# Edges that hold attention steps in chunks 1 to 3, the fifth chunk's scores from chunk 2 on, and coarse pieces of chunk 1 at tiles 1, 3, 5 and 7

## The chip, the cores and the metric

The kernel runs on one core of a Trainium2 chip. The metric is the device time of one execution in microseconds (us). The kernel before takes 1087.3 us, the median of three runs (1086.87, 1087.3 and 1091.65).

## The reference

Two kinds of attention over q, k and v (8 batches, 8 heads, 576 positions, 64 wide) are added, and a gated feed-forward network (FFN) with an RMS norm ahead of it runs on the 4608 tokens.

```
q_d, k_d, v_d = means of q, k, v over 4 neighbours           # 144 positions
out_up    = repeat(softmax(q_d k_d^T / 8) v_d, 4)            # "coarse"
scores    = where(|i - j| < 4, q k^T / 8, -1e9)              # a band, 7 wide
out_local = softmax(scores) v                                # "local"
x   = (out_up + out_local) as [4608, 512]
xn  = x / sqrt(mean(x^2) + 1e-6) * rms_g
g   = xn @ w_gate;  val = xn @ w_val                         # 512 -> 1536
out = (g * sigmoid(g) * val) @ w_out                         # 1536 -> 512
```

## The kernel before, in words

**Chunks and tiles.** The tokens are cut into 18 chunks of 256, numbered 0 to 17. The FFN of a chunk runs in 12 tiles of 128 columns of `w_gate` and `w_val`. "Tile c.f" is tile f of chunk c. Each fp32 operand is split into a high and a low part. For each tile TensorE runs 24 matmuls of the first product (L1344: 12 for `wg`, 12 for `wv`, each four triples of one `xl` and two `xh` matmuls) and, two tiles later, 6 of the second (L1380). Between them stand tanh on ScalarE (L1352), gate (L1355) and product (L1360) on VectorE (DVE), the high part on ScalarE (L1366) and the low part on DVE (L1369). Three buffers `sil` and three `hs` lie between first and second product.

**The input of a chunk.** The tokens of chunks 0 to 2 come from `Dense`, which does the band on TensorE; its root is at L1231 to L1246 and its norm at L1252. The tokens of chunks 3 to 17 come from `Attention`, mostly on DVE. In code order these are its steps:

- eight scores, each a product (L711) and a sum (L715) on DVE, with loads of `q_t` and `kv` on SP's queue (L699, L617);
- the softmax (L732 to L749), with one exponential on ScalarE;
- eight values: the seven neighbours' products are split between ScalarE (L758), DVE and GpSimd (both L765; GpSimd is POOL in the profile), and a sum on DVE (L784);
- twice an "add": `load_up` (L794, two DMAs on ScalarE's queue) brings the coarse result, `add_up` (L800) adds it on DVE, and the squares (L810) run on ScalarE;
- the root: a mean over partitions on TensorE (L817), then eleven or twelve small operations on DVE (L821 to L840) and the norm (L849);
- the turn: transposes on TensorE (L861), and `xh` (L300, ScalarE) and `xl` (L304, DVE), which the first matmul of the next chunk waits for.

**Coarse pieces.** The coarse attention runs in pieces of one batch and one pair of heads. Each has scores on TensorE (L534), maxima, a subtraction and a reciprocal on DVE (L555, L560, L596, L599), exponentials on ScalarE (L565), a turn (L574) and values (L589) on TensorE, and a scale (L603) with a store (L606). Their inputs are summed by chains of accumulating DMAs on GpSimd's queue (L372), which SP loads (L364, L368). Chunk 1 has four pieces, the later ones two each; a piece needs a tile for its scores, and turn and values follow two and three tiles later.

**What sets the order.** Chunk 0 is planned by a planner of its own. Chunks 1 to 17 are emitted by the loop at L1518 to L1559, and a list scheduler orders the instructions of each engine. Within chunk c the loop emits, for each tile, the FFN tile, then queued steps (root at tile 8, turn at tile 10) and coarse pieces, and then the steps of `Attention(c + 1)` whose place in tiles has come (`todo`; scores from 0 to 2.6, softmax at 3.0, values from 3.1 to 6.0, adds at 4.8 and 6.4). What is emitted is free to be placed earlier by the scheduler: nothing but data and buffers holds a step of `todo`. `tc.issue_after(x)` adds an edge: what is traced inside it comes after x on the engines. Before, only queued steps, coarse pieces and second products carry such edges.

In the trace of before, the first matmul of chunk 1 runs at about 145 us; chunks 2, 3 and 4 begin at about 216, 277 and 336.

Of the kernel before, what the change touches and what calls it, by code (L numbers as in the profile page):

```python
# [13 lines left out]
AF = mybir.ActivationFunctionType  # L14
# [15 lines left out]
NF = DF // P  # L30
# [11 lines left out]
FIRST = 1  # L42
WARM = 2
V_ROWS = 50.0
PIECES = {1: (1, 4, 6, 8), 2: (0, 3), 3: (0, 2)}
SUMS = {(1, 6): (3, 0), (1, 11): (3, 2)}


HOP = {"PE": 0.25, "ACT": 0.2, "DVE": 0.15, "POOL": 0.2, "SP": 0.0}
# [127 lines left out]
def attn_moe_kernel(  # L177
# [16 lines left out]
    nc = tc.nc  # L194
# [258 lines left out]
    def behind(ins):  # L453
        return tc.issue_after(ins) if ins else nullcontext()
# [3 lines left out]
    def sums_of(b, hp):  # L458
        if (b, hp // 2) not in sums:
            sums[b, hp // 2] = Sums(b, hp // 2)  # L460
        return sums[b, hp // 2]
# [821 lines left out]
    class Forward:  # L1283
# [6 lines left out]
        def emit(self, f):  # L1290
            self.first(f, 0)
            last = self.first(f, 1)
            self.tanh(f)
            self.gate(f)
            self.product(f)
            self.high(f)
            self.low(f, "DVE")
            return last

        def emit_second(self, f):  # L1300
# [7 lines left out]
        def plan(self, weights, second_weights):  # L1308
            att, c, T = self.att, self.c, due[self.c]
            o_bufs = [buf("ps_o") for _ in range(2)]  # L1310
            last = None
            for f in range(NF):
                at = T + 4.2 * f
                soon = at - SOON
                hp, sil, hs = buf("ps_h"), buf("sil"), buf("hs")
                x = [att.xh_buf, att.xl_buf]
                first = task(
                    "PE", 1.375, lambda f=f: self.first(f, 0), at, [*att.turned, *weights(f)], allocs=[hp], uses=x,
                )
                tanh = task("ACT", 0.38, lambda f=f: self.tanh(f), soon, [first], allocs=[sil], uses=[hp])  # L1320
                val = task("PE", 1.375, lambda f=f: self.first(f, 1), at, [first], uses=[hp, *x])
                gate = task("DVE", 0.415, lambda f=f: self.gate(f), soon, [tanh], uses=[hp, sil])
                prod = task("DVE", 0.415, lambda f=f: self.product(f), soon, [gate, val], uses=[hp, sil])
                high = task("ACT", 0.415, lambda f=f: self.high(f), soon, [prod], allocs=[hs], uses=[sil])
                low = task(
                    (("DVE", 0.42, soon), ("POOL", 0.95, soon)), 0, lambda e, f=f: self.low(f, e), soon, [high], uses=[sil, hs],
                    port=True,
                )
                last = task(
                    "PE", 1.375, lambda f=f: self.second(f), at + 4.2 * LAG, [low, last, *second_weights(f)],  # L1330
                    allocs=o_bufs if f == 0 else [], uses=[hs, *o_bufs],
                )
            for j in range(2):
                o_sb = buf("o_sb")
                copy = task("ACT", 0.6, lambda j=j: self.copy(j), T, [last], allocs=[o_sb], uses=[o_bufs[j]])
                task("SP", 0.1, lambda j=j: self.store(j), T, [copy], uses=[o_sb], dma=0.256 * MB)
# [12 lines left out]

        def tanh(self, f):  # L1350
            self.sil[f] = ffn.tile([P, C], FP32, name="sil", bufs=3)
            nc.scalar.activation(out=self.sil[f], in_=self.p[f][:, 0], func=AF.Tanh, scale=0.5)  # L1352

        def gate(self, f):
            nc.vector.scalar_tensor_tensor(  # L1355
                out=self.sil[f], in0=self.sil[f], scalar=1.0, in1=self.p[f][:, 0], op0=ALU.add, op1=ALU.mult,
            )

        def product(self, f):
            nc.vector.scalar_tensor_tensor(  # L1360
# [39 lines left out]
    for fg in range(3):  # L1400
        for i in range(12):
            if i % 3 == 2 if fg < 2 else i >= 8:
                f = 4 * fg + (i // 3 if fg < 2 else i - 8)
# [94 lines left out]
    early = Dense(2).plan_scores(parts, opening, mask, 24.0, 105.0)  # L1498
# [16 lines left out]

    att, late = atts[FIRST], []  # L1518
    for c in range(FIRST, NCH):
        todo, before, behind_second = [], {}, {}  # L1520
        if c + 1 < NCH:
            nxt = early if c == FIRST else Attention(c + 1)
            todo, queued = nxt.steps()
            todo.sort(key=lambda t: t[0])
            for at, it in zip(PIECES.get(c, (0, 3)), coarse[done:]):
                score, swap, value = Coarse(*it).steps()
                behind_second[at] = score
                before.setdefault(at + 2, []).append(swap)
                before.setdefault(at + 3, []).append(value)
                done += 1  # L1530
            for at, step in queued.items():
                before.setdefault(at, []).append(step)
        fwd = Forward(att)
        for f in range(NF):
            if (c, f) in SUMS:
                sums_of(*SUMS[c, f])
            if f in (0, 6) and c > FIRST:
                for it in coarse[done - 1:done + 1 if f else done]:
                    sums_of(*it)
            last = fwd.emit(f)  # L1540
            for step in before.get(f, ()):
                with behind(last):
                    last = step()
            late.append((fwd, f))
            if len(late) > LAG:
                fw, g = late.pop(0)
                with behind(last if f in before else None):
                    last = fw.emit_second(g)
            if f in behind_second:
                with behind(last):  # L1550
                    behind_second[f]()
            while todo and todo[0][0] < f + 1:
                todo.pop(0)[1]()
        assert not todo
        att = nxt
    assert done == len(coarse)
# [56 lines left out]
```

## Time and profile before

| | us |
|---|---|
| median of three runs | 1087.3 |
| the profiled execution | 1088.73 |
| its span in the profile | 1087.0 |
| outside the span | 1.7 |
| TensorE busy | 1044.5 (96%) |
| DVE busy | 887.4 (82%) |
| ScalarE busy | 626.4 (58%) |
| GpSimd busy | 168.0 (15%) |
| granted TensorE clock, mean | 0.983 |

In the lines of the trace, PE is TensorE, ACT ScalarE, POOL GpSimd and SP the queue of most loads. A line of the timeline has the start (us from the span's start), the busy time, the engine, the source line, the operation, its output and inputs by the program's names, shapes, and how many instructions (x) stand behind one another. In brackets is the idle time ahead of it, and what ended it. A line of the waits has the waiting engine and line, whom it waited for, the sum in us, how often, and the longest. A row of windows has the window, its length, then busy time and count for PE, PEld, DVE, ACT and POOL, the granted clock, DMA share and GB/s.

### The profile page before, as it was taken

To read this page: it belongs to the slowest core of one execution; us is meant where nothing else is said; L and a number is where in the kernel's file an instruction comes from. 1 tells how busy PE (TensorE), PEld (TensorE's weight loads), DVE (VectorE), ACT (ScalarE), POOL (GpSimd) and SP (SyncE) were. 2 spreads that over 40 slices of the span, in tenths; PEclk is the share of its full clock that TensorE was granted. 3 is DMA by queue.
4 is the path that set the end of the run, shared out by engine and by line. 5 is a ranking of instruction groups with operands and counts; after the bars stand their busy time and mean duration, and the time that the engine had idled before them with its cause. 6 is when DMAs were issued, how large, how long until landed. Compare 5 with 4: busy or idle time off the path is not lost.

```text
span 1087.0 us, 23815 instructions
## 1 busy us (share of the span) xinstructions
PE 1044.5 (96%) x8804; PEld 958.7 (88%) x8804; DVE 887.4 (82%) x1988; ACT 626.4 (58%) x2308; POOL 168.0 (15%) x225
## 2 busy tenths in 40 slices
PE   4888899899999999999999999999999999999998
PEld 2667799689998999999999999999999999999997
DVE  5778859885979998989898898989899998986432
ACT  5588743843747483848384838384738383746222
POOL 3201300312121121212121212020202010111000
PEclk8888999999999999999999999999999999999999
DMA  8488842564362635353535353313132222210000
GB/s 264 135 277 309 223 116 75 116 160 83 91 130 63 134 94 118 85 119 87 126 81 123 77 129 81 97 41 106 43 105 61 82 86 65 84 40 21 1 21 20
DMA packets 72731, 113.28 MB, mean 104 GB/s; under 512 B 26006, under 2 KB 33958, under 8 KB 72614
## 3 DMA queue, kind: packets, MB, share of 16 engines
q1 hardware_dynamic: 46342, 91.64, 27.7%
q0 software_dynamic: 8768, 15.95, 9.4%
q10 hardware_dynamic: 17504, 4.16, 1.8%
q8 instruction: 69, 1.13, 0.4%
q14 instruction: 48, 0.39, 0.1%
HBM read 99.92 MB, written 11.80 MB: 103 GB/s over the span
## 4 chain that ended last, share of the span: by engine, by line
PE 81%; DVE 9%; DMA 4%; ACT 3%; issue 2%; SPq 0%; ACTq 0%; POOL 0%; DVEq 0%; POOLq 0%
PE ps_h L1344 48%; PE ps_o L1380 25%; PE ps_a L589 2%; DVE prod L711 1%; PE ps_a L534 1%; PE ps_a L861 1%; DMA qk<-in_qk_sum_dram 1%; PE ps_a L574 1%; DVE sc L715 1%; ACT a_g L565 1%; DMA vs<-in_v_sum_dram 1%; DVE sil L1355 1%; DVE x_t L784 1%; DVE sil L1360 1%; DMA wo<-in_qk_sum_dram 1%
## 5 line engine op out<-in xcount | busy, mean ns | idle before, releaser
L1380 PE MATMUL ps_o<-wo,hs 128*128 128x512 f32 x1296 | 336.0, 397 | 0.9 <-DVE hs L1369 0.9
L1344 PE MATMUL ps_h<-xh,wg 128*128 128x256 f32 x1728 | 314.3, 279 | 0.0
L1344 PE MATMUL ps_h<-xh,wv 128*128 128x256 f32 x1728 | 310.0, 277 | 0.0
L1344 PEld LDWEIGHTS ps_h<-xh,wg 128*128 128x128 f32 x1728 | 267.1, 190 | 5.9 <-issue 0.4
L1344 PEld LDWEIGHTS ps_h<-xh,wv 128*128 128x128 f32 x1728 | 263.8, 188 | 3.4 <-issue 0.2
L1380 PEld LDWEIGHTS ps_o<-wo,hs 128*128 128x128 f32 x1296 | 228.9, 188 | 39.0 <-DVE hs L1369 1.1
L758 ACT ACTIVATE prod<-kv,sc 128x64 f32<-128x64 f32 x960 | 247.8, 427 | 16.0 <-DVE sc L749 11.3
L1344 PE MATMUL ps_h<-xl,wg 128*128 128x256 f32 x864 | 243.2, 282 | 7.8 <-DVE sil L1360 5.5
L1344 PE MATMUL ps_h<-xl,wv 128*128 128x256 f32 x864 | 241.5, 279 | 3.8 <-DVE sil L1355 3.8
L1352 ACT ACTIVATE sil<-ps_h 128x256 f32<-128x256 f32 x216 | 83.5, 387 | 224.7 <-PE ps_h L1344 205.8
L1344 PEld LDWEIGHTS ps_h<-xl,wg 128*128 128x128 f32 x864 | 163.8, 190 | 14.6 <-DVE sil L1360 6.6
L1344 PEld LDWEIGHTS ps_h<-xl,wv 128*128 128x128 f32 x864 | 162.4, 188 | 8.6 <-DVE sil L1355 4.8
L1366 ACT ACTIVATE hs<-sil 128x256 fp32r<-128x256 f32 x216 | 90.0, 418 | 132.4 <-DVE sil L1360 108.9
L765 POOL TENSOR_TENSOR prod<-sc,kv 128x256 f32<-128x256 f32 x120 | 92.3, 808 | 402.8 <-DVE sc L749 175.5
L784 DVE TENSOR_REDUCE x_t<-prod 128x128 f32<-128x896 f32 x120 | 127.4, 1073 | 20.9 <-PE ps_a L861 14.2
L1355 DVE SCALAR_TENSOR_TENSOR sil<-sil,ps_h 128x256 f32<-128x256 f32 x216 | 89.5, 414 | 61.6 <-ACT sil L1352 56.3
L711 DVE TENSOR_TENSOR prod<-q_t,kv 128x896 f32<-128x896 f32 x120 | 129.7, 1083 | 1.4 <-DMA kv<-in_k_pad_dram 1.2
L715 DVE TENSOR_REDUCE sc<-prod 128x14 f32<-128x896 f32 x120 | 128.2, 1075 | 0.0
L1369 DVE TENSOR_TENSOR hs<-sil,hs 128x256 fp32r<-128x256 f32 x213 | 93.4, 439 | 33.2 <-ACT hs L1366 33.1
L1360 DVE SCALAR_TENSOR_TENSOR sil<-sil,ps_h 128x256 f32<-128x256 f32 x216 | 89.3, 414 | 5.9 <-PE ps_h L1344 4.5
L372 POOL DMA_DIRECT2D qk<-in_qk_sum_dram x36 | 32.4, 900 | 253.4 <-DMA qk<-in_qk_sum_dram 222.2
L765 DVE TENSOR_TENSOR prod<-sc,kv 128x128 f32<-128x128 f32 x120 | 53.6, 467 | 0.7
(187 smaller groups left out, 940.8 us busy)
## 6 DMA issues: line engine op xcount, KB each, us to landing
kv<-in_k_pad_dram SPq DMA_DIRECT2D x60, 320.0 KB
kv<-in_v_pad_dram SPq DMA_DIRECT2D x60, 320.0 KB
qk<-in_qk_sum_dram POOLq DMA_DIRECT2D x36, 288.0 KB, 5.0
q_t<-in_q_band_dram SPq DMA_DIRECT2D x60, 128.0 KB
out_dram<-o_sb SPq DMA_DIRECT2D x30, 256.0 KB
vs<-in_v_sum_dram POOLq DMA_DIRECT2D x36, 144.0 KB, 3.4
qk<-in_qk_sum_dram SPq DMA_DIRECT2D x12, 288.0 KB
wo<-in_qk_sum_dram SPq DMA_DIRECT2D x2, 1152.0 KB
```

The source lines that it names most:

```text
L711: nc.vector.tensor_tensor(out=pr, in0=bcast(q[:, s0:s0 + 2], 2, NO), in1=window(k, s0), op=ALU.mult)
L715: nc.vector.tensor_reduce(out=self.sc[:, j, par, s0:s0 + 2], in_=self.pr[i], axis=AX.X, op=ALU.add,)
L758: nc.scalar.activation(out=self.pr[i][:, o, s], in_=self.v[j, par][:, s0 + s + o], func=AF.Copy, scale=p[:, s, o:o + 1],)
L765: (nc.vector if engine == "DVE" else nc.gpsimd).tensor_tensor(out=self.pr[i][:, a:b], in0=bcast(p[:, :, a:b].rearrange("p s o -> p o s"), ...
L784: nc.vector.tensor_reduce(out=self.x[j][:, s0:s0 + 2, par], in_=pr.rearrange("p o s d -> p s d o"), axis=AX.X, op=ALU.add,)
L1344: last = nc.tensor.matmul(out=self.p[f][:, t], lhsT=wi(f)[:, 0, k], rhs=xi[:, k], start=(n == 0), stop=(n == 3 * KT - 1),).ins
L1352: nc.scalar.activation(out=self.sil[f], in_=self.p[f][:, 0], func=AF.Tanh, scale=0.5)
L1355: nc.vector.scalar_tensor_tensor(out=self.sil[f], in0=self.sil[f], scalar=1.0, in1=self.p[f][:, 0], op0=ALU.add, op1=ALU.mult,)
L1360: nc.vector.scalar_tensor_tensor(out=self.sil[f], in0=self.sil[f], scalar=0.5, in1=self.p[f][:, 1], op0=ALU.mult, op1=ALU.mult,)
L1366: nc.scalar.activation(out=self.hs[f][:, 0], in_=self.sil[f], func=AF.Copy)
L1369: (nc.gpsimd if engine == "POOL" else nc.vector).tensor_tensor(out=self.hs[f][:, 1], in0=self.sil[f], in1=self.hs[f][:, 0], op=ALU.subtract,)
L1380: last = nc.tensor.matmul(out=self.o[j], lhsT=lhs[:, cols], rhs=rhs(f)[:, 0], start=(f == 0 and i == 0), stop=(f == NF - 1 and i == 2),).ins
```

## The change

Three tables change and one mechanism comes in.

- `PIECES[1]`: the four coarse pieces of chunk 1 start at tiles 1, 3, 5 and 7 in place of 1, 4, 6 and 8. `SUMS` asks for the last sums one tile earlier.
- `AHEAD` gives `Attention(3)` and `Attention(4)` places of their own, in tiles from the start of the chunk before theirs: first score and spacing, softmax, first value and spacing, the two adds. A negative place lies in the chunk before that, so the scores of chunk 3 are traced from tile 1.2 on and those of chunk 4 (the fifth chunk) from tile 2.7 on.
- In chunks 1 to 3 (`c < HELD`) each step of `todo` is traced inside two edges, one behind the current tile's gate (DVE) and one behind its tanh (ScalarE). The steps of `Attention(5)` and later are traced in chunk 4 and later, and carry no such edge.

```diff
@@ -42,8 +42,13 @@
 FIRST = 1
 WARM = 2
 V_ROWS = 50.0
-PIECES = {1: (1, 4, 6, 8), 2: (0, 3), 3: (0, 2)}
-SUMS = {(1, 6): (3, 0), (1, 11): (3, 2)}
+PIECES = {1: (1, 3, 5, 7), 2: (0, 3), 3: (0, 2)}
+SUMS = {(1, 6): (3, 0), (1, 10): (3, 2)}
+AHEAD = {
+    3: (-9.5, 1.0, 0.9, 1.0, 0.65, 3.7, 6.3),
+    4: (-5.0, 0.95, 2.7, 2.8, 0.6, 5.0, 7.0),
+}
+HELD = max(AHEAD)
 
 
 HOP = {"PE": 0.25, "ACT": 0.2, "DVE": 0.15, "POOL": 0.2, "SP": 0.0}
@@ -1295,6 +1300,7 @@
             self.product(f)
             self.high(f)
             self.low(f, "DVE")
+            self.marks = self.gated, self.tanhed
             return last
 
         def emit_second(self, f):
@@ -1349,12 +1355,12 @@
 
         def tanh(self, f):
             self.sil[f] = ffn.tile([P, C], FP32, name="sil", bufs=3)
-            nc.scalar.activation(out=self.sil[f], in_=self.p[f][:, 0], func=AF.Tanh, scale=0.5)
+            self.tanhed = nc.scalar.activation(out=self.sil[f], in_=self.p[f][:, 0], func=AF.Tanh, scale=0.5).ins
 
         def gate(self, f):
-            nc.vector.scalar_tensor_tensor(
+            self.gated = nc.vector.scalar_tensor_tensor(
                 out=self.sil[f], in0=self.sil[f], scalar=1.0, in1=self.p[f][:, 0], op0=ALU.add, op1=ALU.mult,
-            )
+            ).ins
 
         def product(self, f):
             nc.vector.scalar_tensor_tensor(
@@ -1515,12 +1521,24 @@
 
 
 
+    def placed(att, todo):
+        if att.c not in AHEAD:
+            return todo
+        s0, ds, soft, v0, dv, *adds = AHEAD[att.c]
+        at = [s0 + ds * i for i in range(8)] + [soft] + [v0 + dv * i for i in range(8)] + adds
+        return [(t, step) for t, (_, step) in zip(at, todo)]
+
+    made = {}
     att, late = atts[FIRST], []
     for c in range(FIRST, NCH):
         todo, before, behind_second = [], {}, {}
         if c + 1 < NCH:
-            nxt = early if c == FIRST else Attention(c + 1)
+            nxt = early if c == FIRST else made.get(c + 1) or Attention(c + 1)
             todo, queued = nxt.steps()
+            todo = [(at - (c - nxt.c + 1) * NF, step) for at, step in placed(nxt, todo) if at >= 0]
+            if c + 2 in AHEAD:
+                made[c + 2] = Attention(c + 2)
+                todo += [(at + NF, step) for at, step in placed(made[c + 2], made[c + 2].steps()[0]) if at < 0]
             todo.sort(key=lambda t: t[0])
             for at, it in zip(PIECES.get(c, (0, 3)), coarse[done:]):
                 score, swap, value = Coarse(*it).steps()
@@ -1550,7 +1568,10 @@
                 with behind(last):
                     behind_second[f]()
             while todo and todo[0][0] < f + 1:
-                todo.pop(0)[1]()
+                with ExitStack() as held:
+                    for mark in fwd.marks if c < HELD else ():
+                        held.enter_context(tc.issue_after(mark))
+                    todo.pop(0)[1]()
         assert not todo
         att = nxt
     assert done == len(coarse)
```

Lines of the new file stand five or six higher in number: L711 is L716, L715 is L720, L821 is L826, L838 to L840 are L843 to L845, L849 is L854, L861 is L866, L1355 is L1361, L1360 is L1366, L1369 is L1375, L1344 is L1350.

What this does to the order of the instructions shows best on DVE, in two places. The first is DVE in chunk 1, in the middle of the root of chunk 2's tokens (`newton`, `rinv`, `rms`). In these rows `prod` and `sc` are the scores of chunk 3, and `sil` and `hs` the FFN's gate, product and low part. Before:

```order
L1355 SCALAR_TENSOR_TENSOR sil<-sil,ps_h 128x256
L1244 SCALAR_TENSOR_TENSOR newton<-rinv 128x2
L711 TENSOR_TENSOR prod<-q_t,kv 128x896
L1360 SCALAR_TENSOR_TENSOR sil<-sil,ps_h 128x256
L1245 TENSOR_TENSOR newton<-newton,rms 128x2
L711 TENSOR_TENSOR prod<-q_t,kv 128x896
L715 TENSOR_REDUCE sc<-prod 128x14
L1246 SCALAR_TENSOR_TENSOR rinv<-newton,rinv 128x2
L1369 TENSOR_TENSOR hs<-sil,hs 128x256
L1355 SCALAR_TENSOR_TENSOR sil<-sil,ps_h 128x256
```

The same place in the new order:

```order
L1361 SCALAR_TENSOR_TENSOR sil<-sil,ps_h 128x256
L1249 SCALAR_TENSOR_TENSOR newton<-rinv 128x2
L1366 SCALAR_TENSOR_TENSOR sil<-sil,ps_h 128x256
L1250 TENSOR_TENSOR newton<-newton,rms 128x2
L1251 SCALAR_TENSOR_TENSOR rinv<-newton,rinv 128x2
L1257 TENSOR_SCALAR x_t<-ps_a,rinv 128x256 x2
L1375 TENSOR_TENSOR hs<-sil,hs 128x256
L1361 SCALAR_TENSOR_TENSOR sil<-sil,ps_h 128x256
L716 TENSOR_TENSOR prod<-q_t,kv 128x896
L1366 SCALAR_TENSOR_TENSOR sil<-sil,ps_h 128x256
L720 TENSOR_REDUCE sc<-prod 128x14
L1375 TENSOR_TENSOR hs<-sil,hs 128x256
```

The scores have moved behind the norm (L1257), and then come one product and one sum to a tile.

The second place is DVE at the end of chunk 3, at the root of chunk 4's tokens (`rms`, `rinv`, `newton` with 8 columns). Here `prod` and `sc` in the new order are the scores of chunk 5. Before, from the root's first operation on:

```order
L821 TENSOR_SCALAR rms<-ps_a 128x8
L825 TENSOR_SCALAR rinv<-rms 128x8
L829 TENSOR_SCALAR rinv<-rinv 128x8
L838 SCALAR_TENSOR_TENSOR newton<-rinv 128x8
L839 TENSOR_TENSOR newton<-newton,rms 128x8
L840 SCALAR_TENSOR_TENSOR rinv<-newton,rinv 128x8
L838 SCALAR_TENSOR_TENSOR newton<-rinv 128x8
L1369 TENSOR_TENSOR hs<-sil,hs 128x256
```

Six more rows of before lead to the norm (L849), one of them a low part (L1369). The new order from the root's first operation on:

```order
L826 TENSOR_SCALAR rms<-ps_a 128x8
L716 TENSOR_TENSOR prod<-q_t,kv 128x896
L1361 SCALAR_TENSOR_TENSOR sil<-sil,ps_h 128x256
L1366 SCALAR_TENSOR_TENSOR sil<-sil,ps_h 128x256
L1375 TENSOR_TENSOR hs<-sil,hs 128x256
L716 TENSOR_TENSOR prod<-q_t,kv 128x896
L830 TENSOR_SCALAR rinv<-rms 128x8
L720 TENSOR_REDUCE sc<-prod 128x14
L1366 SCALAR_TENSOR_TENSOR sil<-sil,ps_h 128x256
L1375 TENSOR_TENSOR hs<-sil,hs 128x256
L720 TENSOR_REDUCE sc<-prod 128x14
L834 TENSOR_SCALAR rinv<-rinv 128x8
```

Between this first operation and the norm (L854) the new order has in all five products and five sums of scores, two gates, three products and three low parts of the FFN, four operations of chunk 5's softmax, and the eleven others of the root. Before, there are two low parts and the eleven others of the root.

## The prediction

> **What bounds the kernel now.** I read the page first: TensorE's row of the span in 40 slices (a digit is the busy share in tenths).
>
> ```profile
> PE   4888899899999999999999999999999999999998
> ```
>
> From a quarter of the span on TensorE is busy nine tenths and more: it is the bound. So an edit of chunks 1 to 3 is worth what it takes from TensorE's waits there, less what it adds. The waits of TensorE from 130 to 395 us (chunk 1 to chunk 4) are these (us in total, times, longest):
>
> ```profile
> PE ps_h L1344 <- DVE sil L1360: 5.5, 3, 4.9
> PE ps_a L574 <- ACT a_g L565: 0.9, 2, 0.7
> PE ps_a L861 <- DVE x_t L849: 0.4, 1, 0.4
> PE ps_h L1344 <- DVE sil L1355: 0.2, 1, 0.2
> PE ps_h L1344 <- DVE xl L304: 0.2, 1, 0.2
> ```
>
> They sum to 7.2 us, and one of them is 4.9. The timeline of TensorE shows it, and what follows it:
>
> ```profile
> 188.60 3.00 PE L1380 MATMUL ps_o<-wo,hs 128*128 128x512 f32 x12
> ...
> 197.17 0.58 PE L1344 MATMUL ps_h<-xl,wg 128*128 128x256 f32 x1 [4.93 <-DVE sil L1360]
> ...
> 200.44 0.28 PE L1344 MATMUL ps_h<-xl,wv 128*128 128x256 f32 x1
> ...
> 200.78 0.28 PE L1344 MATMUL ps_h<-xl,wv 128*128 128x256 f32 x1
> ```
>
> A triple (one xl, two xh matmuls) takes 0.34 us from 200.44 on (200.78 - 200.44), so 0.113 a matmul; one of the second product takes 0.25 (twelve in 3.00). From 197.17 to 200.44 there are 15 of them in 3.27 us, where 15 x 0.113 = 1.70 would do: after a wait of this length the slow restart costs another 1.6. So 7.2 + 1.6 = **8.8 us** is all that the edit can win, 0.8% of the time.
>
> Why DVE was late there: the timeline of DVE in chunk 1.
>
> ```profile
> 157.30 0.16 DVE L1231 TENSOR_TENSOR rms<-ss 128x2 f32<-128x2 f32 x1 [4.53 <-ACT x_t L1222]
> ...
> 171.80 0.41 DVE L1355 SCALAR_TENSOR_TENSOR sil<-sil,ps_h 128x256 f32<-128x256 f32 x1
> 172.13 1.08 DVE L711 TENSOR_TENSOR prod<-q_t,kv 128x896 f32<-128x896 f32 x1
> ...
> 176.20 0.87 DVE L1252 TENSOR_SCALAR x_t<-ps_a,rinv 128x256 f32<-128x256 f32 x2
> ...
> 179.37 2.08 DVE L711 TENSOR_TENSOR prod<-q_t,kv 128x896 f32<-128x896 f32 x2
> ...
> 192.28 0.82 DVE L555 TENSOR_REDUCE m_g<-ps_a 72x2 f32<-72x288 f32 x2
> 193.02 1.07 DVE L784 TENSOR_REDUCE x_t<-prod 128x128 f32<-128x896 f32 x1
> 194.01 0.41 DVE L1369 TENSOR_TENSOR hs<-sil,hs 128x256 fp32r<-128x256 f32 x1
> ```
>
> DVE works strictly in its order. Of chunk 3's scores it ran six products and most of their sums between the root's first operation (157.3) and its norm (176.2): 19 us for a chain of a dozen small operations. The gates and products of the FFN came late behind them. The rows give the prices that I use: a score product or sum 1.00 us (two in 2.08), a value sum 1.0 (193.02 to 194.01), a gate, product or low part 0.33 (171.80 to 172.13), the two maxima of a coarse piece 0.74 (192.28 to 193.02).
>
> **The change, part by part.**
>
> *Chunk 1 (held scores; coarse pieces at 1, 3, 5, 7).* The order now puts one score product and one sum per FFN tile behind that tile's gate: 2.0 + 3 x 0.33 = 3.0 us, and on every other tile a coarse piece (0.74 for the maxima, with its four small operations some 1.5). TensorE has 24 x 0.113 + 6 x 0.25 = 4.2 us a tile. DVE keeps up, and the 4.93 wait with its restart goes: 4.9 + 1.6, -6.5. The moved pieces cost TensorE the same work as before. The four moved score loads and the sums' loads on SP stand behind buffers that are freed earlier than needed; I cost them at 0.
>
> *Chunk 2 (values of chunk 3, then six of the eight scores of chunk 4).* Here the held steps leave DVE idle, since nothing may be pulled forward any more. New waits on DVE, each with its nearest row:
>
> ```profile
> DVE x_t L784 <- POOL prod L765: 4.0, 1, 4.0
> DVE z_g L596 <- ACT a_g L565: 1.9, 2, 1.7
> DVE x_t L800 <- DMA up_t<-up: 1.1, 1, 1.1
> qk<-in_qk_sum_dram POOLq DMA_DIRECT2D x36, 288.0 KB, 5.0
> ```
>
> And two stretches of before, the first mostly chunk 2, the second chunk 3; DVE's busy time is the third pair of columns:
>
> ```profile
> 205.00:275.00 70.00, 69.08 (x552) 62.82 (x552) 50.76 (x113) 33.33 (x130) 18.41 (x23) 1.00 0.55 117
> 277.00:331.00 54.00, 53.19 (x421) 49.17 (x421) 46.98 (x105) 28.62 (x114) 9.70 (x12) 1.00 0.47 109
> ```
>
> In four places of chunks 1 and 2 the reciprocal of a coarse piece (L596) now follows its scale with nothing between, and DVE waits for four exponentials: 4 x 1.7 = 6.8. GpSimd's share of the values (L765) stands between accumulating DMAs on its queue, each held until the one before has landed (5.0): I take one wait like the 4.0. The loads of the coarse sum (add's DMAs on ACT's queue) are held behind tanh too, so add_up waits for them: 1.1 or more. Sum 11.9 us of DVE, much of it in time that DVE has to spare: in the first stretch of before it was busy 50.8 of 70 us.
>
> The Trainium skill's page DMA: Bandwidth & Descriptors, section Anatomy of one DMA, gives 2.0 us plus bytes over 436 GB/s; an estimate by it for 288 KB is 2.7. The row says 5.0 and decides. By the page GpSimd's queue would keep ahead, the 4.0 would fall away, and the total below would come out about 4 us lower, at 1093.
>
> *The boundary of chunk 3 and 4.* This is the term that decides. In the trace of before, DVE's root and norm of chunk 4's tokens, and TensorE from the mean (L817) to the turn (L861):
>
> ```profile
> 326.44 0.16 DVE L821 TENSOR_SCALAR rms<-ps_a 128x8 f32<-128x8 f32 x1
> ...
> 329.29 1.28 DVE L849 TENSOR_TENSOR x_t<-x_t,rinv 128x512 f32<-128x512 f32 x2
> ```
>
> ```profile
> 324.82 0.28 PE L817 MATMUL ps_a<-ss,same_sb 128*128 128x8 f32 x2
> 324.95 3.02 PE L1380 MATMUL ps_o<-wo,hs 128*128 128x512 f32 x12
> 327.81 0.28 PE L1344 MATMUL ps_h<-xl,wg 128*128 128x256 f32 x1
> ...
> 330.12 1.23 PE L861 MATMUL ps_a<-ident_sb,x_t 128*128 128x128 f32 x8 [0.43 <-DVE x_t L849]
> ```
>
> The root took DVE 2.9 us, and the turn (L861) waited 0.43. In the new order the scores of chunk 5, which no edge holds, stand inside this root. Between its first operation and the norm: 10 score products and sums x 1.00, 8 FFN operations x 0.33 = 2.6, four softmax operations and the root's own eleven at about 0.15 to 0.2 (2.5 together), half of the norm 0.6: **15.7 us**. TensorE has, from the mean to the turn, 12 matmuls of the second product and 24 of the first: 2.9 (324.95 to 327.81) is what before spent on the former, 24 x 0.113 = 2.7 on the latter, 5.6. Everything behind the turn on TensorE is kept there by an edge. So the turn waits at least 15.7 - 5.6 = **10.1**, and a slow restart of 1.6 follows: +11.7. Against -8.8 that is **+2.9 as the best case**.
>
> It gets worse if DVE is late when the mean is done. From the xl of chunk 3 (L304) to this norm the new order holds two score products, two sums, and two value sums more than before, and small ones for 0.3: 4.0 + 2.0 + 0.3, **6.3 us**. Before, DVE idled 7.0 of 54 us in chunk 3 (46.98 busy), among them the wait of 1.1 for a load that the new order has as well. I take none of it as usable: the turn comes 6.3 later after chunk 3's first matmul than before. That matmul can start at most 5.9 earlier (7.9 of the gains lie ahead of it, and 2.0 of TensorE work, the moved coarse matmuls, is moved ahead of it); with the 11.9 of new waits I take 1.0. So the turn moves by 6.3 - 1.0 = +5.3 (bounds: +1.3, the best case without restart, and +8), and with the restart by **+6.9**.
>
> *Chunk 4.* ScalarE now has five value products of chunk 5 still ahead of it when chunk 4's xh is done; by the chain of waits of before five take 1.36:
>
> ```profile
> 320.05 1.36 ACT prod L758 x5
> ```
>
> The first coarse piece's exponentials (1.7) stand behind them, and TensorE's coarse turn behind those: I take a wait of 1.3 + 1.7 = 3 (bounds 0, if the seven matmul groups ahead cover it, and 4). From chunk 6 on the orders are the same, and TensorE has no spare time to win anything back.
>
> **Sum.** The profiled execution took 1088.7 (span 1087.0, 1.7 outside), 1.4 above the median of the runs shown, 1087.3. +6.9 + 3 = +9.9; I forecast the median at 1087.3 + 9.9 = 1097.2, call it **1097**.
>
> **Rivals.**
>
> *A: only the root's wait.* DVE reaches the root as soon as the mean is done and chunk 4's wait is hidden: +2.9, **1090**. It is not slower by more than can be told. It decides at DVE's first root operation of chunk 4: if it starts within half a microsecond of the mean, A holds. For it: DVE's 19 idle us in the first stretch of before. Against: the 6.3 us of work put off into chunk 3.
>
> *B: the change does as it says.* The scores no longer delay the FFN and no new wait appears: -8.8, 1078.5. It needs DVE to pass 33 operations in 5.6 us, against the prices above.
>
> *C: GpSimd's queue.* In chunk 3 the values' fourth GpSimd part stands behind two landings of accumulating DMAs; at 5.0 each it comes about 4 us late, and everything behind it on DVE, the root included: another +4 to +6 on the forecast, **1102**.
>
> *D: the hold binds nothing*, because the scheduler placed the steps there anyway: the orders differ, so it has no chance.
>
> **Chances.** Forecast 0.55, A 0.18, B 0.05, C 0.22. A measurement of this kernel tells about 0.5% (5.4 us) from no change. Faster is B, 0.05. Same is most of A, 0.15. Slower is the rest, 0.80. The range leaves out B and the ends: low 1090.5 (A with a little lateness), high 1105 (C).
>
> **What would show it.** Right: no wait near 197; one wait of 10 to 16 us at L861 of chunk 4 (L866 in the new file), ended by the norm; matmuls of 0.21 behind it; DVE without a pause from the root's first operation to the norm. Wrong: a wait at that turn under 5 us, or new waits at other turns; a loss that grows after chunk 6 would speak for a cause that I do not see.

## The result, and the profile after

The changed kernel takes 1100.09 us, the median of six runs (1097.01 to 1105.01); the kernel before took 1087.88 us in six runs beside it (1086.87 to 1091.65). The ratio is 1.0111, with a 95% interval of 1.0083 to 1.0139: slower by 12.2 us, 1.1%. The profiled execution took 1099.6 us with a span of 1097.8, so 10.8 of span are to be found in the trace.

TensorE's row of the 40 slices shows where they are:

```profile
PE   4888899989986999999999999999999999999998
```

One slice, the thirteenth (329 to 357 us), fell to 6; before there was a 9. The waits of TensorE from 130 to 410 us (us in total, times, longest):

```profile
PE ps_a L866 <- DVE x_t L854: 11.2, 1, 11.2
PE ps_o L1386 <- DVE hs L1375: 2.6, 2, 1.8
PE ps_a L822 <- ACT up_t L815: 1.5, 1, 1.5
PE ps_a L579 <- ACT a_g L570: 1.2, 1, 1.2
PE ps_h L1350 <- DVE xl L309: 0.3, 1, 0.3
PE ps_h L1350 <- DVE sil L1361: 0.2, 1, 0.2
```

The wait of 4.9 us at a product of chunk 1 is gone. One wait of 11.2 us has come, at the turn of chunk 4's tokens, and five small kinds of 5.8 in sum. After 410 us the view of the waits lists none for TensorE, as before. The timeline of TensorE from the mean of chunk 4's tokens (L822) past their turn (L866) to chunk 4's first matmul:

```profile
321.24 0.39 PE L822 MATMUL ps_a<-ss,same_sb 128*128 128x8 f32 x2 [1.55 <-ACT up_t L815]
321.49 3.01 PE L1386 MATMUL ps_o<-wo,hs 128*128 128x512 f32 x12
...
326.85 0.39 PE L1350 MATMUL ps_h<-xh,wv 128*128 128x256 f32 x2
338.47 1.94 PE L866 MATMUL ps_a<-ident_sb,x_t 128*128 128x128 f32 x8 [11.23 <-DVE x_t L854]
340.06 5.68 PE L1386 MATMUL ps_o<-wo,hs 128*128 128x512 f32 x18
345.67 0.71 PE L539 MATMUL ps_a<-qk 64*72 64x144 f32 x8
346.31 0.38 PE L1350 MATMUL ps_h<-xl,wg 128*128 128x256 f32 x1
```

The mean ran at 321.24, 3.6 us earlier than before (324.82), but the turn 8.35 later (338.47 against 330.12). Behind it the same 18 matmuls of the second product took 5.6 us (340.06 to 345.67) in place of 4.3: the slow restart. The same rows before:

```profile
331.10 4.38 PE L1380 MATMUL ps_o<-wo,hs 128*128 128x512 f32 x18
335.41 0.71 PE L534 MATMUL ps_a<-qk 64*72 64x144 f32 x8
```

On the other side of the wait stands DVE's timeline:

```profile
323.03 0.15 DVE L826 TENSOR_SCALAR rms<-ps_a 128x8 f32<-128x8 f32 x1
323.10 1.08 DVE L716 TENSOR_TENSOR prod<-q_t,kv 128x896 f32<-128x896 f32 x1
...
331.98 2.07 DVE L720 TENSOR_REDUCE sc<-prod 128x14 f32<-128x896 f32 x2
...
334.04 1.08 DVE L716 TENSOR_TENSOR prod<-q_t,kv 128x896 f32<-128x896 f32 x1
...
337.64 1.28 DVE L854 TENSOR_TENSOR x_t<-x_t,rinv 128x512 f32<-128x512 f32 x2
340.89 1.13 DVE L309 SCALAR_TENSOR_TENSOR xl<-ps_a,g_sb,xh 128x128 fp32r<-128x128 f32 x4 [0.83 <-ACT xh L305]
```

From the root's first operation (323.03) to its norm (337.64) DVE pauses nowhere for more than 0.1 us, and ten of the operations there are score products and sums of chunk 5. Before, the same stretch took 2.9 us.

### The profile page after: what moved, and what is told of

Read it like the earlier page. It is cut to its first block, busy times and chain, and to the rows that moved or that the text cites. A ratio compares the mean times of both kernels' runs of the same rounds, so it can differ in the third digit from the quotient of the medians.

```text
span 1097.8 us, 23811 instructions
## 1 busy us (share of the span) xinstructions
PE 1045.2 (95%) x8804; PEld 959.4 (87%) x8804; DVE 889.0 (81%) x1988; ACT 627.1 (57%) x2308; POOL 167.4 (15%) x225
## 4 chain that ended last, share of the span: by engine, by line
PE 81%; DVE 7%; DMA 5%; ACT 4%; issue 2%; SPq 0%; POOL 0%; ACTq 0%; DVEq 0%; POOLq 0%
PE ps_h L1350 49%; PE ps_o L1386 24%; DMA qk<-in_qk_sum_dram 2%; PE ps_a L594 2%; PE ps_a L539 2%; PE ps_a L866 1%; DMA vs<-in_v_sum_dram 1%; PE ps_a L579 1%; ACT a_g L570 1%; DMA up_t<-up 1%; DVE prod L716 1%; DVE sc L720 1%; ACT prod L763 1%; DMA wo<-in_qk_sum_dram 1%; DVE sil L1361 0%
## 5 line engine op out<-in xcount | busy, mean ns | idle before, releaser
L1350 PE MATMUL ps_h<-xh,wg 128*128 128x256 f32 x1728 | 313.5, 279 | 0.0
L1350 PE MATMUL ps_h<-xh,wv 128*128 128x256 f32 x1728 | 310.4, 277 | 0.0
L1350 PEld LDWEIGHTS ps_h<-xh,wg 128*128 128x128 f32 x1728 | 266.1, 189 | 6.4 <-issue 1.0
L1350 PEld LDWEIGHTS ps_h<-xh,wv 128*128 128x128 f32 x1728 | 263.8, 188 | 3.8 <-issue 0.4
L1350 PE MATMUL ps_h<-xl,wv 128*128 128x256 f32 x864 | 241.2, 279 | 3.8 <-DVE sil L1361 3.8
L1350 PE MATMUL ps_h<-xl,wg 128*128 128x256 f32 x864 | 242.5, 281 | 2.5 <-DVE xl L309 2.5
L1350 PEld LDWEIGHTS ps_h<-xl,wg 128*128 128x128 f32 x864 | 163.2, 189 | 8.3 <-issue 3.4
L1350 PEld LDWEIGHTS ps_h<-xl,wv 128*128 128x128 f32 x864 | 162.2, 188 | 8.4 <-DVE sil L1361 4.8
L789 DVE TENSOR_REDUCE x_t<-prod 128x128 f32<-128x896 f32 x120 | 127.6, 1074 | 28.5 <-POOL prod L770 11.5
L1361 DVE SCALAR_TENSOR_TENSOR sil<-sil,ps_h 128x256 f32<-128x256 f32 x216 | 89.5, 415 | 65.4 <-ACT sil L1358 60.2
L716 DVE TENSOR_TENSOR prod<-q_t,kv 128x896 f32<-128x896 f32 x120 | 129.7, 1083 | 0.2
L720 DVE TENSOR_REDUCE sc<-prod 128x14 f32<-128x896 f32 x120 | 128.3, 1074 | 0.0
L1375 DVE TENSOR_TENSOR hs<-sil,hs 128x256 fp32r<-128x256 f32 x213 | 91.8, 432 | 30.2 <-ACT hs L1372 30.0
L1366 DVE SCALAR_TENSOR_TENSOR sil<-sil,ps_h 128x256 f32<-128x256 f32 x216 | 89.2, 413 | 5.8 <-PE ps_h L1350 4.6
L770 DVE TENSOR_TENSOR prod<-sc,kv 128x128 f32<-128x128 f32 x120 | 56.4, 494 | 0.5
```

The source lines that it names most:

```text
L716: nc.vector.tensor_tensor(out=pr, in0=bcast(q[:, s0:s0 + 2], 2, NO), in1=window(k, s0), op=ALU.mult)
L720: nc.vector.tensor_reduce(out=self.sc[:, j, par, s0:s0 + 2], in_=self.pr[i], axis=AX.X, op=ALU.add,)
L770: (nc.vector if engine == "DVE" else nc.gpsimd).tensor_tensor(out=self.pr[i][:, a:b], in0=bcast(p[:, :, a:b].rearrange("p s o -> p o s"), ...
L789: nc.vector.tensor_reduce(out=self.x[j][:, s0:s0 + 2, par], in_=pr.rearrange("p o s d -> p s d o"), axis=AX.X, op=ALU.add,)
L1350: last = nc.tensor.matmul(out=self.p[f][:, t], lhsT=wi(f)[:, 0, k], rhs=xi[:, k], start=(n == 0), stop=(n == 3 * KT - 1),).ins
L1361: self.gated = nc.vector.scalar_tensor_tensor(out=self.sil[f], in0=self.sil[f], scalar=1.0, in1=self.p[f][:, 0], op0=ALU.add, op1=ALU.mult ...
```

## The experiments

Three numbers are read from every trace at a turn. *Late* is the time from the mean on TensorE to the root's first operation on DVE. *Stretch* is the time from there to the middle of the norm (its start plus 0.6). *Cover* is what TensorE still works between mean and turn. The sum late + stretch - cover should be the wait. With all three read from a trace this is bookkeeping; a test is how near a stretch comes that was worked out from an order before it ran. *Idle* is DVE's idle time from 150 us to the mean of chunk 4's tokens. Times are compared as ratios to the kernel before, run beside each, since its single runs alone spread by 1% (1083.0 to 1095.3 in one set).

### The scores put behind the root

```diff
+    normed = {}
...
                 if s0 == 0:
                     self.load_score(j, par)
-                self.score(i)
-                self.score_sum(i)
+                with behind(normed[4]) if self.c == 5 and i >= 3 else nullcontext():
+                    self.score(i)
+                    self.score_sum(i)
...
-            nc.vector.tensor_tensor(
+            normed[self.c] = nc.vector.tensor_tensor(
...
-            )
+            ).ins
```

> The changed kernel, with the last five scores of chunk 5 (product and sum) put behind the norm of chunk 4's tokens by one more edge. The new order has no score in that root any more, but four products and five sums in the next one, of chunk 5's tokens: 36 operations there, by the prices of the prediction 9 x 1.0 + 10 x 0.33 + 17 x 0.165 + 0.6 = 15.7 us, against 12 and 48 matmuls on TensorE, 8.4 us. Theory (a turn waits for what stands in DVE's root): the 11.2 us wait at the turn of chunk 4's tokens falls below 2, a new one of about 7.3 stands at the turn of chunk 5's tokens, and the time is about 1097. Rival (the put-off work of DVE costs its whole price wherever it stands): 1100, no change. Were the place alone at fault, with room for the scores later: 1088.

Ratio 1.0135 (1.0101 to 1.0168), median 1103.1. TensorE's timeline has both turns, that of chunk 4's tokens and that of chunk 5's:

```profile
329.48 1.23 PE L869 MATMUL ps_a<-ident_sb,x_t 128*128 128x128 f32 x8 [1.68 <-DVE x_t L857]
...
397.54 1.94 PE L869 MATMUL ps_a<-ident_sb,x_t 128*128 128x128 f32 x8 [9.64 <-DVE x_t L857]
```

The first half of the theory holds: with the scores out of the root its wait falls from 11.23 to 1.68. The hope of a cheaper place does not. The work stands in the next root, DVE comes 2.8 us late to it, and the price is paid there. The time is above the rival's 1100 and further still above the theory's 1097.

### The scores left out

```diff
+                if self.c == 5 and i >= 3:
+                    return
                 self.score(i)
                 self.score_sum(i)
...
                 self.sc = band.tile([P, 2, 2, US, NO], FP32, name="sc")
+                if self.c == 5:
+                    nc.gpsimd.memset(self.sc, 0.0)
```

> The changed kernel, with the products and sums of the last five of chunk 5's eight scores left out (their place in the score tile is set to zero by GpSimd); loads and all else stay. Theory (the scores in the root are the loss): the wait at the turn of chunk 4's tokens falls from 11.2 to under 2, none takes its place at chunk 5's, and the time is that of the changed kernel less 11.2 and the slow restart of 1.9, 1085 to 1088. Rival (the held steps of chunks 1 and 2 and GpSimd's queue cost the time, and the turn only collects it): the waits of DVE in chunks 2 and 3 stay, some other wait of TensorE ends last, and the time stays above 1093.

This kernel leaves out ten of DVE's operations, five products and five sums. Ratio 1.0009 (0.9982 to 1.0036): by the ratios about 11 us under the changed kernel, and just over the time expected. Its waits of TensorE from 130 to 460 us:

```profile
PE ps_a L870 <- DVE x_t L858: 3.0, 1, 3.0
PE ps_o L1390 <- DVE hs L1379: 2.2, 2, 2.0
```

Taking 10 us of DVE's work away takes about as much off the time: DVE is what is behind. The turn still waits 3.0, more than the 2 expected, since chunk 5's softmax and value products now stand in the root (27 operations); and with the edges in place nothing is won against the kernel before.

### The places without the edges, and the pieces alone

```diff
-HELD = max(AHEAD)
+HELD = 0
```

> The changed kernel without its edges on the steps of attention; the new places (table of places, coarse pieces at 1, 3, 5, 7, sums at 10) stay. Both roots are free of scores in its order. Theory (the loss comes from the edges, by way of the root): no wait over 1 us at the turn of chunk 4's tokens, a wait of several us in chunk 1 as before, time 1085 to 1090. Rival (the places and the moved pieces cost the time): 1096 or more.

The second kernel drops the places too, and keeps the moved pieces:

```diff
-AHEAD = {
-    3: (-9.5, 1.0, 0.9, 1.0, 0.65, 3.7, 6.3),
-    4: (-5.0, 0.95, 2.7, 2.8, 0.6, 5.0, 7.0),
-}
-HELD = max(AHEAD)
+AHEAD = {}
+HELD = 0
```

> The kernel before with the coarse pieces of chunk 1 at 1, 3, 5, 7 and the last sums at 10, and nothing else of the change. Theory (without edges the score products still run ahead in chunk 1): waits of TensorE of 4 to 7 us in chunk 1 as before, at the gates or at the coarse turns, time within 3 us of the kernel before. Rival (the moved pieces by themselves take the wait away): 1081 to 1085.

Ratios 0.9999 (0.9970 to 1.0027) and 0.9987 (0.9958 to 1.0016). In both the 4.9 us wait is gone and another has come in its place. The waits of TensorE without the edges:

```profile
PE ps_a L579 <- ACT a_g L570: 5.9, 3, 2.2
```

and with the pieces alone:

```profile
PE ps_a L576 <- ACT a_g L567: 5.4, 3, 2.1
```

Three coarse turns now wait about 2 us each for ScalarE's exponentials. None of this makes the kernel slower, so with these places and pieces the loss comes with the edges.

### Edges in chunk 1 alone

```diff
 AHEAD = {
     3: (-9.5, 1.0, 0.9, 1.0, 0.65, 3.7, 6.3),
-    4: (-5.0, 0.95, 2.7, 2.8, 0.6, 5.0, 7.0),
 }
-HELD = max(AHEAD)
+HELD = 2
```

> The changed kernel with the edges in chunk 1 alone, and a place of its own for chunk 3's attention alone; from chunk 2 on the steps are free again. Its order has no score in any root of chunks 3 to 6. Theory (the loss is a root's, and the edges as such win the 4.9 us wait with its restart): that wait is gone, no turn waits over 2 us, time 1081 to 1085. Rival (what the edges put off out of chunk 1 costs its price in chunks 2 and 3 whatever the order): 1088 to 1092.

Ratio 0.9971 (0.9953 to 0.9988). Its waits of TensorE:

```profile
PE ps_h L1349 <- DVE sil L1365: 1.5, 1, 1.5
PE ps_a L821 <- ACT up_t L814: 1.4, 1, 1.4
PE ps_a L865 <- DVE x_t L853: 0.5, 1, 0.5
```

The long wait is gone and no turn pays for it; the median, 1085.2, is at the upper end of what the theory expected. The same kernel once more, with more rounds:

> The kernel with edges in chunk 1 alone and places for chunk 3's attention alone, once more and with more rounds. Theory: DVE idles no longer up to the mean of chunk 4's tokens than in the kernel before (36.7 against 36.6 us) and the 4.9 us wait is gone, so it is 0.2 to 0.5% faster. Rival (its first result was within the spread): ratio 0.9985 to 1.002.

Ratio 0.9982 (0.9961 to 1.0004), between what theory and rival gave. The two agree on a gain of 0.2 to 0.3%; the second interval just takes in no change, so the gain is likely and small. With the old places of the coarse pieces:

```diff
-PIECES = {1: (1, 3, 5, 7), 2: (0, 3), 3: (0, 2)}
-SUMS = {(1, 6): (3, 0), (1, 10): (3, 2)}
+PIECES = {1: (1, 4, 6, 8), 2: (0, 3), 3: (0, 2)}
+SUMS = {(1, 6): (3, 0), (1, 11): (3, 2)}
```

> The kernel with edges in chunk 1 alone and places for chunk 3's attention, but with the coarse pieces at 1, 4, 6, 8 and the sums at 11 as in the kernel before. Theory (the edges make the gain, not the pieces): the 4.9 us wait is gone, time as with the moved pieces, 0.3% under the kernel before. Rival (two pieces close together need DVE and ScalarE in the same tiles, with or without edges): waits of 2 us and more at a coarse turn or a gate in chunk 1, and no gain.

Ratio 0.9983 (0.9958 to 1.0009). No wait at a gate, product or coarse turn of chunk 1 is over 0.2 us, so the edges take the wait away with either set of pieces. A wait of 1.6 at chunk 3's first xl is new. Which pieces are better can't be told from these intervals.

### Edges in chunks 1 and 2, and in chunks 1 and 3

```diff
-HELD = max(AHEAD)
+HELD = 3
```

> The changed kernel with its edges in chunks 1 and 2 only, no longer in chunk 3. Its order has two products and three sums of chunk 5's scores in the root of chunk 4's tokens, where the changed kernel has five and five; 32 operations, by the same prices 5 x 1.0 + 8 x 0.33 + 21 x 0.165 + 0.6 = 11.4 us against 15.2 measured. Theory (the wait is what stands in the root less TensorE's cover of 5.6): a wait of 6 to 8 us at the turn of chunk 4's tokens, time 4 us under the changed kernel, 1096. Rival (the edges in chunk 3 start the loss): no wait over 2 us there, 1085 to 1088.

Ratio 1.0073 (1.0043 to 1.0104), and at the turn of chunk 4's tokens

```profile
337.07 1.08 PE L866 MATMUL ps_a<-ident_sb,x_t 128*128 128x128 f32 x4 [8.12 <-DVE x_t L854]
```

Half as many scores in the root, and a stretch of 11.07 (11.4 expected). The wait is 8.12, just above the 6 to 8 expected, because DVE came 2.4 us late to the root and not 1.8. The other pair of chunks:

```diff
-                    for mark in fwd.marks if c < HELD else ():
+                    for mark in fwd.marks if c in (1, 3) else ():
```

> The changed kernel with its edges in chunks 1 and 3, not in chunk 2. Its order still has five products and five sums in the root of chunk 4's tokens, 33 operations as the changed kernel, and no score in the root of chunk 3's. Theory (the root's stretch less the cover is the wait, wherever the edges are that led to it): late by 1.8, 15.2 long, cover 5.9, so a wait of about 11 at the turn of chunk 4's tokens; chunk 3 begins 3 to 7 us earlier than in the kernel before, so the time is 1092 to 1097. Rival (the edges in chunk 2, with DVE's idle time there, are the loss, and the root only shows it): no wait over 4 us at that turn, 1084 to 1089.

Ratio 1.0066 (1.0040 to 1.0092), median 1095.3:

```profile
335.53 1.73 PE L866 MATMUL ps_a<-ident_sb,x_t 128*128 128x128 f32 x7 [10.44 <-DVE x_t L854]
```

As the theory has it: five products and five sums in the root make a wait of 10 to 11 us, whichever edges brought them there. It costs less in the end: chunk 3 began earlier, with its first matmul at 272.40 us, against 275.34 in the changed kernel and 276.82 before, and the span is 2.7 us under the changed kernel's (1095.1 against 1097.8). In chunk 3 DVE waits nowhere for GpSimd here, so the long wait at the turn doesn't need such a wait.

### GpSimd taken out of chunk 4's values

```diff
+            np_ = 0 if c == 4 else np_
...
-                self.value(i, "POOL", NO - self.np, NO)
+                if self.np:
+                    self.value(i, "POOL", NO - self.np, NO)
```

> The changed kernel with GpSimd's two of seven neighbours of chunk 4's value products given to DVE. The root of chunk 4's tokens still holds five products and five sums of scores. Theory (the root decides): DVE's wait of 4.4 us for GpSimd in chunk 3 is gone, eight products on DVE are some 0.35 longer each (2.8 together), the wait at the turn stays between 9 and 12, time 0 to 2 us under the changed kernel, 1098 to 1100. Rival C of the prediction (GpSimd's queue makes DVE late, and the turn collects it): 4 to 6 us under it, 1094 to 1096.

In the changed kernel DVE waits for GpSimd four times between 140 and 420 us, where before it waited once, 4.0 us:

```profile
DVE x_t L789 <- POOL prod L770: 11.5, 4, 4.4
```

One of the four lies in chunk 3, and GpSimd's timeline shows what rival C of the prediction said: two accumulating DMAs, each held until the one before had landed, stand ahead of the product that DVE waits for.

```profile
297.74 0.89 POOL L377 DMA_DIRECT2D qk<-in_qk_sum_dram  x1 [2.99 <-DMA qk<-in_qk_sum_dram]
302.50 0.87 POOL L377 DMA_DIRECT2D qk<-in_qk_sum_dram  x1 [3.87 <-DMA qk<-in_qk_sum_dram]
303.06 1.60 POOL L770 TENSOR_TENSOR prod<-sc,kv 128x256 f32<-128x256 f32 x2
```

```profile
304.10 1.09 DVE L789 TENSOR_REDUCE x_t<-prod 128x128 f32<-128x896 f32 x1 [4.37 <-POOL prod L770]
```

With chunk 4's share on DVE this wait is gone, and the ratio is 1.0101 (1.0069 to 1.0133), against 1.0111. TensorE's waits:

```profile
PE ps_a L868 <- DVE x_t L856: 11.7, 1, 11.7
```

The turn waits as long as ever, so the scores in the root are enough for the long wait. But the run prices the wait for GpSimd badly: it takes 4.4 us of waiting from DVE and gives it 2.4 us of work (its eight value products take 6.8 us in place of 4.4). Rival C's 4 to 6 us did not count that work, and the 2 us that are left can't be told from the spread. C's mechanism was there; what it costs by itself stays open.

### The scores split over two roots

The edit is that of the scores put behind the root, with 6 in place of 3:

```diff
...
+                with behind(normed[4]) if self.c == 5 and i >= 6 else nullcontext():
...
```

> The changed kernel with only the last two scores of chunk 5 behind the norm of chunk 4's tokens. Its order has three products and three sums in the root of chunk 4's tokens (25 operations) and three and three in that of chunk 5's (37 operations, with 18 and 72 matmuls on TensorE between mean and turn). Theory (wait = lateness + stretch - cover): 1.8 + 11.0 - 5.9 = 6.9 at the first turn and 2 + 14.0 - 12.6 = 3.4 at the second; the put-off work is paid once in sum, time 1098 to 1100. Rival (a score in a root is free as long as some of TensorE's cover is left, so that two covers carry it): the second turn waits under 1, time 1094 to 1096.

Ratio 1.0132 (1.0098 to 1.0167). The two turns:

```profile
336.61 1.94 PE L869 MATMUL ps_a<-ident_sb,x_t 128*128 128x128 f32 x8 [5.96 <-DVE x_t L857]
...
397.96 0.63 PE L869 MATMUL ps_a<-ident_sb,x_t 128*128 128x128 f32 x4 [3.59 <-DVE x_t L857]
```

Both waits are near what was worked out (6.9 and 3.4). TensorE now runs slow three times instead of once, behind these two waits and behind one of 1.55 us ahead of them (last section). The median, 1102.8, is above the 1098 to 1100 expected, and the time is again no better than the changed kernel's.

### Edges on the scores alone, in chunks 1 and 2

`scoring` is true for the steps of the eight scores.

```diff
-HELD = max(AHEAD)
+HELD = 3
...
-                    for mark in fwd.marks if c < HELD else ():
+                    for mark in fwd.marks if c < HELD and scoring(todo[0][1]) else ():
```

> The changed kernel with edges on the score steps alone, in chunks 1 and 2 alone; softmax, values and adds are free. Its order has six products and five sums (of chunk 4's scores) in the root of chunk 3's tokens, 34 operations against 12 and 72 matmuls of cover, and none and one in the root of chunk 4's. Theory (wait = lateness + stretch - cover): 1.5 + 17.2 - 11.1 = 7.6 at the turn of chunk 3's tokens, under 2 at chunk 4's; with a restart of 1.9 and the gain of 6.5 in chunk 1, 1090 to 1092. Rival (the root of chunk 4's tokens alone is dear): no wait over 2 us at any turn, 1081 to 1085.

```profile
277.18 1.09 PE L868 MATMUL ps_a<-ident_sb,x_t 128*128 128x128 f32 x4 [7.59 <-DVE x_t L856]
```

The wait that was worked out as 7.6 is 7.59, at another turn, with another cover. The time is not: ratio 1.0086 (1.0055 to 1.0118), 1098 where 1090 to 1092 was expected. That time counted the 6.5 us won in chunk 1 as still in hand. Chunk 2's first tanh came only 1.9 us earlier (217.1 us against 219.0 before), but a tanh's place depends on the order too, so where the rest went isn't shown.

### What they say together

For the turn of chunk 4's tokens, unless another chunk is named (us):

| kernel | late | stretch | cover | sum | wait | idle | ratio |
|---|---|---|---|---|---|---|---|
| before | 1.62 | 3.45 | 4.87 | 0.2 | 0.43 | 36.8 | 1 |
| pieces alone | 1.63 | 3.45 | 4.87 | 0.2 | 0.44 | 38.1 | 0.9987 |
| places without edges | 1.18 | 3.45 | 4.86 | -0.2 | none | 37.3 | 0.9999 |
| edges in chunk 1 | 2.06 | 4.45 | 6.22 | 0.3 | 0.52 | 36.7 | 0.9971 |
| edges in chunks 1, 3 | 0.89 | 15.20 | 5.89 | 10.2 | 10.44 | 44.8 | 1.0066 |
| edges in chunks 1, 2 | 2.44 | 11.07 | 6.00 | 7.5 | 8.12 | 47.2 | 1.0073 |
| GpSimd out | 2.50 | 14.87 | 5.89 | 11.5 | 11.71 | 47.0 | 1.0101 |
| the change | 1.79 | 15.21 | 6.00 | 11.0 | 11.23 | 50.1 | 1.0111 |
| split, chunk 4 | 1.77 | 11.53 | 7.58 | 5.7 | 5.96 | 52.2 | 1.0132 |
| split, chunk 5 | 0.84 | 14.90 | 12.75 | 3.0 | 3.59 | | |
| scores behind the root, chunk 5 | 2.78 | 15.43 | 8.75 | 9.5 | 9.64 | 51.1 | 1.0135 |
| scores held, chunk 3 | 1.49 | 17.22 | 11.35 | 7.4 | 7.59 | | 1.0086 |

The sum gives every wait to within 0.65 us, and always a little too little. The stretches, worked out beforehand from the orders, came within 0.9 us: 15.7, 11.4, 11.0, 14.0, 15.7 and 17.2 expected, 15.2, 11.1, 11.5, 14.9, 15.4 and 17.2 measured. The lateness was not worked out but taken from earlier traces; with scores in this root it was between 0.89 and 2.50. And the kernels fall into two groups: where DVE idles 36 to 38 us up to that mean the time is that of before or a little better; where it idles 45 to 52 the time is 0.7 to 1.4% longer. (The kernel with scores left out idles 51.2 as well, but has 10 us less to do and isn't in the table. The last row's idle time isn't given, since a long wait lies ahead of that mean.) The rows of the stretches, before and after (DVE's busy time is the third pair of columns):

```profile
150.00:324.82 174.82, 168.22 (x1426) 153.20 (x1425) 138.06 (x301) 91.48 (x359) 33.88 (x42) 0.99 0.49 112
```

```profile
150.00:321.24 171.24, 165.50 (x1396) 150.44 (x1385) 121.15 (x277) 88.11 (x340) 31.98 (x40) 1.00 0.47 105
```

and with edges in chunk 1 alone:

```profile
150.00:318.69 168.69, 165.69 (x1412) 151.03 (x1411) 131.96 (x298) 89.40 (x349) 32.86 (x42) 1.00 0.52 115
```

The changed kernel reaches the mean with 16.9 us less of DVE's work done than before (121.15 against 138.06), and with 13.3 more idled away (50.1 against 36.8). My reading is that this is a debt: edges let nothing be pulled forward, DVE idles, and the work comes due in the next root that no edge protects, where TensorE waits for it.

## Why the prediction was right

The sign, the place and the mechanism of the wait were right: TensorE waits at the turn of chunk 4's tokens for a root full of scores. The time, 1097 against 1100.1 measured, came near in part by luck, as the steps show.

- **The wait of 4.9 us and its restart go**: right. The rows of 143 to 200 us, before and after, have TensorE busy for 51.85 and for 57.00 us:

```profile
143.00:200.00 57.00, 51.85 (x497) 47.08 (x496) 43.99 (x100) 26.60 (x99) 4.84 (x6) 0.97 0.35 90
```

```profile
143.00:200.00 57.00, 57.00 (x555) 51.65 (x555) 38.70 (x92) 20.89 (x72) 2.67 (x3) 1.00 0.40 96
```

- **Chunk 3 starts 1.0 us earlier**: nearly right, 1.5 (275.34 against 276.82). The rest of the gain is lost on the way, in waits of 1.80, 1.23 and 0.84 us at second products and a coarse turn of chunk 2, and in matmuls that now stand ahead of it (from 143 us on 56 of the coarse scores in place of 48).
- **The root's stretch and the wait**: 15.7 forecast, 15.2 measured; TensorE's cover was 6.0 where 5.6 was forecast. So the floor for the wait is 9.2 and not 10.1, and the lateness of 1.8 makes it 11.0 of the 11.23 measured.
- **The turn comes 5.3 later**: it came 8.35 later, a little beyond the bound of 8. The step that failed is "the turn comes 6.3 later after chunk 3's first matmul than before". From that matmul to the turn it is 63.1 us against 53.3, 9.8 more and not 6.3. In this stretch DVE works 7.1 us more (53.40 against 46.28) and idles 2.7 more (9.73 against 7.02), where the forecast let its idle time stay as it was. The longest of its waits there is the 4.37 for GpSimd, which the prediction had left to rival C.
- **The restart**: 1.6 forecast; eight turn matmuls and 18 of the second product took 7.2 us in place of 5.3, so 1.9.
- **Chunk 4, +3**: wrong. From chunk 4's first matmul (+10.25, 346.31 against 336.06) to the end of the span (+10.8) it is 0.55. No coarse turn of chunk 4 waits: it is the prediction's lower bound.
- The sum in the trace is 8.35 + 1.9 + 0.55 = 10.8, forecast 5.3 + 1.6 + 3 = 9.9. Two errors, 3.1 too little at the turn and 2.5 too much in chunk 4, nearly cancel; that is the luck.
- **Rival A** (2.9) fell. It counted 11.7 for the new wait and its restart, where the trace has 13.1, and none of the other waits, which sum to 5.8. Its sign, DVE at the root within half a microsecond of the mean, decides little: DVE came 1.79 us late, but 1.62 before the change too. On chunk 4 A was right.
- **Rival C** had a true mechanism, the wait of 4.37 us behind two landings in chunk 3, and its 1102 is nearer to the measured 1100.1 than the forecast's 1097. The run without GpSimd can't price it, and the run with edges in chunks 1 and 3 shows that the long wait stands without it. So C adds to the forecast's mechanism and doesn't replace it; by how much isn't shown.
- The 4 us by which the total would be lower by the Trainium skill's page DMA: Bandwidth & Descriptors (Anatomy of one DMA) did not show. The changed kernel's row of DMA issues has 4.6 us for the 288 KB, far nearer to the 5.0 of before than to the page's 2.7:

```profile
qk<-in_qk_sum_dram POOLq DMA_DIRECT2D x36, 288.0 KB, 4.6
```

  What faster landings would be worth, no run here tells.

What the prediction took as the cause, scores in a root, is the form of the loss and not its size. That was shown by moving them out (1.0135), splitting them (1.0132) and leaving them out (1.0009). That DVE's idle time is what grows into the debt rests on the two groups of the table, and every kernel of the dear group has edges beyond chunk 1. No kernel here kept all edges and filled the idle time, and none took off only one of the two edges, behind gate or behind tanh, so that much is argued and not shown.

## What to carry to other kernels

An edge that holds work back on a busy engine can cost more than the wait that it removes is worth: add up that engine's idle time and the work put off, up to the next hand-over. At each hand-over the other engine waits late + stretch - cover. Stretch and cover can be worked out from an order before anything runs; the lateness can't, and the time of the kernel needs the waits ahead of the hand-over too. Hold back as little as the one wait needs (here chunk 1's steps) and leave the rest free.

## What the runs showed of the hardware

After every one of the nine waits of TensorE of 3.6 us or more (3.59 to 11.71) that these traces hold from 130 to 470 us, the granted clock in the 4 us from the wait's end was 0.50 to 0.63. After the 33 waits of 0.97 to 2.96 us it was 1.00, but for two: 2.00 us where the scores were left out (0.63), and 1.55 us in the split kernel (0.60). There, twelve matmuls of the second product behind the mean ran slow, and the stretch up to the turn's wait took 7.5 us:

```profile
323.07:330.60 7.53, 7.53 (x38) 6.47 (x38) 7.53 (x15) 1.22 (x3) 0.00 (x0) 0.77 0.31 90
```

The changed kernel had the same wait of 1.55 us at the same place, and the same 38 matmuls took 6.0:

```profile
321.24:327.24 6.00, 5.99 (x38) 5.29 (x38) 6.00 (x13) 1.22 (x3) 0.00 (x0) 1.00 0.32 91
```

So a wait of 1.5 to 2 us may or may not cost a restart; what decides between them, these traces don't show. The Trainium skill's page TensorE: Matmul & The Clock Gate, Part 1, has the clock fall after at least one idle window of about 3.4 us. The nine long waits agree; the two short ones, 1.55 and 2.00 us, are shorter than such a window, and here the measurement decides.
